# Two layers of linear attention and squared-ReLU FFN on one core: b2 as a weight row, squares on ACT, 32-blocked features, a sum by accumulating DMA, re-placed weight preparation

## The chip, the cores and the metric

The kernel runs on one NeuronCore of a Trainium2 chip. The metric is the device time of one execution in microseconds; the median of three runs of the kernel before is 1429.65 us (1428.79 to 1433.52).

The engines are TensorE (PE, with its weight loads PEld), VectorE (DVE), ScalarE (ACT), GpSimd (POOL) and SyncE (SP, which here only issues DMAs). Each takes its instructions in order; they wait for one another through semaphores.

## The reference

Two layers over x of 2048 tokens by 640 features. One layer is

```python
phi = lambda t: where(t > 0, t + 1, exp(t)) + 1e-6
q, k, v = layernorm(x) @ wqkv            # 32 heads of 20
kv, z = phi(k)^T v, sum_s phi(k)         # per head, over all 2048 tokens
x = x + (phi(q) kv / (phi(q) . z + 1e-6)) @ wo
h = layernorm(x) @ w1 + b1               # 640 -> 1728
x = x + relu(h)**2 @ w2 + b2             # 1728 -> 640
```

Both layers use the same weights, all in float32.

## The kernel before, in words

**Precision.** Every float32 operand of a large product is split into a high part (rounded by an ACT copy to fp32r) and a low part (a DVE subtract); a product is then three fp32r matmuls (`mm3`, L456 to L460). `split` (L121) is the pair of instructions. Splitting is therefore most of the work of ACT and DVE.

**Attention, first stage of a layer** (the loop at L783). The 2048 tokens are 16 tiles of 128. For tile t, x is normalized (`ln_stats`, `ln_apply`; the inverse root is two small POOL instructions, L362 and L363), brought into the transposed layout with the features on the partitions, split (`xT_split`), and multiplied by the resident weights of k and q (`part`, L538). The `Phi` class computes phi: exp on ACT (L555), two DVE instructions for the rest (L562, L563), into a tile from a pool `r` of three buffers. `k_post` (L746) splits phi(k) (low half on DVE at L756) and adds it to the running sum `acc` on POOL (L753; the first tile is a copy, L751). The products with x accumulate in PSUM (`g_part`, `gt_part`). phi(q) is stored to DRAM. For the tiles in `LATE` phi(q) is computed after the loop, in the gaps of the next stage, so these tiles take one `r` buffer instead of two.

**Weight preparation, layer 0 only.** The FFN's weights are split once, stored to DRAM (`kept`), and read from there in both layers. `Prep` (L229) does it inside the attention loop: `load` brings 14 chunks of w1 ("a") and 7 pairs of row tiles of w2 ("t") as scheduled in `PREP`; `mix` (L265, POOL) forms the combinations of w2 that the Winograd form of Strassen's product needs; `high` (ACT, L290) and `low` (DVE, L296) split; `store` (SP, L305, L310) writes the halves. `prep_step` runs four times per tile. The buffers are `g` (raw, four of them) and `u` (split; a ring of six that later holds the FFN weights in flight).

**Middle.** The per-head matrices are formed and multiplied with wo into M; the first four tiles of the attention's output are computed, added to x, normalized and transposed (`x_turned`, `f_trans`), so that the first group of the FFN can start.

**FFN** (the loop at L1388), in four groups g of 512 tokens. FC1 is 14 chunks c of 128 hidden features (`fc1`, L1131), each 15 matmuls into one of four PSUM banks in turn (10 for the last chunk). `act` (L1150) adds b1 and applies ReLU on ACT (L1155) and squares on DVE (L1156) into the array R. Chunk 13 packs the 64 remaining features with their low-order weights. FC2 multiplies R by w2 with seven products instead of eight (`ORDER`, 28 steps n of about 12 matmuls, L1212). `s_op` combines quarters of R in place (DVE, L1173); `u_hi` and `u_lo` split each factor into an arena of five slots (ACT L1192, DVE L1196); `fc2_add` adds finished partial results from PSUM to x (DVE, L1225). The FFN weights stream through the ring `u`, SP loading one when a slot is used up; seven of them (`load_stay`) stay for the layer.

**Side work in the FFN.** While group g is in the FFN, the attention's output for the four tiles of group g+1 is computed by `single(g, i)` (L1276), with its parts placed as events: denominators and scaling on DVE (L689 to L702), a 32x32 block transpose (DVE, L417), 16 block moves (ACT, L426), a split (L1239, L1241), the output product (PE, `out`, into banks 6 and 7, after the chunks in `OUTS`), the residual add (DVE, L1313), statistics and layernorm, a trip through DRAM that does the rest of the transpose (POOL-issued store L389, SP loads L398, DVE `turn` L407), and a split into xTb (`x_split`). `f_bias` (L733) adds b2 to x with a POOL instruction (L736).

**What sets the order.** The schedule is manual: each engine's order is the order in which the code calls. In the FFN it is set by `events`, a table keyed by (g, position) with lists of functions; positions 0 to 13 are the FC1 chunks and 14 + n the FC2 steps. Functions of one position run in the order in which they were registered; before, `single` registers first, then `ffn_events`, then `side_last`.

Of the kernel before, what the change touches and what calls it, by code (L numbers as in the profile page):

```python
# [13 lines left out]
P = 128  # L14
S, D, F = 2048, 640, 1728
H, DH = 32, 20
NT = S // P
# [27 lines left out]
PREP = {2: "aaa", 3: "t", 4: "t", 5: "aaaa", 6: "t", 7: "t", 8: "aaaa", 9: "t", 10: "t", 11: "aaa", 12: "t"}  # L45
# [6 lines left out]
F_BUFS, X_BUFS = 8, 4  # L52
# [12 lines left out]
def kernel(  # L65
# [37 lines left out]
    b2bc = cpool.tile([P, D], F32, name="b2bc")  # L103
    b1sb = cpool.tile([P, NF], F32, name="b1sb")

    def late_consts():
        nc.sync.dma_start(
            b2bc, bass.AP(tensor=b2.tensor, offset=b2.offset, ap=[[0, P], [1, D]])
        )
# [119 lines left out]
    class Prep:  # L229
# [19 lines left out]
        def load_t(self, p):  # L249
            a, b, q = gtile("wa"), gtile("wb"), gtile("wq")  # L250
# [122 lines left out]

    def of_chunk(v, c):

        return v.rearrange("t (p c) -> t c p", c=DC)[:, c]
# [27 lines left out]
    def turn(z):  # L404

        y = ftile("y")
        nc.vector.transpose(  # L407
            out=y.rearrange("p (c i q) -> p i c q", c=DC, q=B32),
            in_=z.rearrange("p (i q c) -> p i c q", c=DC, q=B32),
        )  # L410
        return y
# [100 lines left out]
    for layer in range(N_LAYERS):  # L512
# [213 lines left out]
        def b_x1(t, ps):  # L726
            v = halves_sb(xr[t])
            nc.vector.tensor_tensor(out=v, in0=halves(ps), in1=v, op=ALU.add)
            ln_stats(("b", t), xr[t])
            xn[t] = ftile("xn")  # L730
            ln_apply(("b", t), xn[t], xr[t])

        def f_bias(t):  # L733

            v = xr[t]
            nc.gpsimd.tensor_tensor(out=v, in0=v, in1=b2bc, op=ALU.add)  # L736
# [9 lines left out]
        def k_post(t, r, between=()):  # L746

            kh[t] = u = xtile("kh")
            nc.scalar.activation(u[:, 0], r, AF.Copy)
            if t == 0:  # L750
                nc.gpsimd.tensor_copy(acc, r)  # L751
            else:
                nc.gpsimd.tensor_tensor(out=acc, in0=acc, in1=r, op=ALU.add)  # L753
            for f in between:
                f()
            nc.vector.tensor_tensor(out=u[:, 1], in0=r, in1=u[:, 0].bitcast(F32), op=ALU.subtract)  # L756
# [6 lines left out]
        def x_end(t):  # L763
            return yza.pop(t)[1] if layer == 0 else turn(yza.pop(t))
# [7 lines left out]
        def prep_step(t, i):  # L772
            if layer == 0 and t in PREP_AT:
                if i == 0:
                    prep.mix()
                prep.low()
                prep.high()
                if i == 3:
                    prep.load(PREP.get(t + 1, ""))

        late = LATE[layer]
        q_end = None
        for t in range(NT):  # L783
# [14 lines left out]
            if first:  # L798
# [38 lines left out]
                nc.sync.dma_start(pqd[0], fq.r)  # L837
                continue
# [33 lines left out]
            if early:  # L872
                xT_split(2, turn(yz0[2]))
# [196 lines left out]
        def f_trans(t, ps):  # L1070
            transpose_x(ps, xn.pop(t))
            f_split(t, ps)
# [10 lines left out]
        def x_turned(i):  # L1083

            b_x1(i, po[i])
            yzx[i] = blocks_x(xn.pop(i))
            side_work.extend(lambda k=k: turn_move(yzx[i], (k,)) for k in range(JQ))
            side_work.append(lambda: f_split(i, yzx.pop(i)[1]))
# [9 lines left out]
        wu.free = 3  # L1098
# [27 lines left out]
        nc.gpsimd.memset(R[FL:, :, 1, KH - 1], 0.0)  # L1126
        x1_odd["tile"] = bp.tile([P, TG, D], F32, name="x1", tag="x1", bufs=1)
# [22 lines left out]
        def act(c, ps):  # L1150
# [3 lines left out]
            if c < 13:  # L1154
                nc.scalar.activation(r, v, AF.Relu, bias=b1sb[:, c : c + 1])  # L1155
                nc.vector.tensor_tensor(out=r, in0=r, in1=r, op=ALU.mult)  # L1156
# [119 lines left out]
        def single(g, i):  # L1276
# [3 lines left out]
            def on(n, f):  # L1280
                if n < 0 and g > 0:
                    at(g - 1, NF + N_STEPS + 2 * n, f)
                elif n >= NF:
                    at(g, NF + 2 * (n - NF), f)
                else:
                    at(g, max(n, 0), f)
# [9 lines left out]
            on(b - 3, lambda: next(sp, None))  # L1296
# [13 lines left out]
            def add():  # L1310
# [3 lines left out]
                ln_stats(("b", t), xr[t])  # L1314
                xn[t] = ftile("xn")
                ln_apply(("b", t), xn[t], xr[t])

            at(g, ("pe", b), out)
            on(b + 1, add)

            def store():
                xd[t] = spread_out(xn.pop(t))

            on(b + 1, store)
            on(b + 2, lambda: f_bias(t))
# [8 lines left out]
        def ffn_events(g):  # L1334
            for k in range(PAIRS):
                at(g, 6 + k, lambda k=k: u_hi(g, k))
                at(g, 6 + k, lambda k=k: u_lo(g, k))
            for k in range(3):
                at(g, 9 + 2 * k, lambda k=k: s_op(1, k))
                at(g, NF + k, lambda k=k: s_op(2, k))  # L1340
            at(g, 11, lambda: u_hi(g, PAIRS))
            at(g, 11, lambda: u_lo(g, PAIRS))
            s = NF
            at(g, s, lambda: s_op(1, 3))
            at(g, s + 3, lambda: s_op(2, 3))
            for n in range(PAIRS + 1, N_STEPS):
                at(g, s + n - 4, lambda n=n: u_hi(g, n))
                at(g, s + n - 4, lambda n=n: u_lo(g, n))
            for k in range(PAIRS):
                at(g, s + 6 + k, lambda k=k: s_op(3, k))  # L1350
                at(g, s + 11 + k, lambda k=k: s_op(4, k))
            for q in range(len(ORDER) - 1):
                for i in range(2):
                    at(g, s + PAIRS * (q + 1) + i, lambda q=q, i=i: fc2_add(g, q, i))

        def side_last():
# [20 lines left out]
            for t in range(2):  # L1377
                at(g, s + 8 + 4 * t, lambda t=t: xT_split(t, turn(yz0[t])))

        for g in range(NG):  # L1380
            if g < NG - 1:
                for i in range(TG):
                    single(g, i)
        for g in range(NG):
            ffn_events(g)
        side_last()

        for g in range(NG):  # L1388
            for c in range(NF):
# [5 lines left out]
                if g == 0 and c < TG:  # L1395
                    f_bias(c)
# [50 lines left out]
```

## Time and profile before

| | |
|---|---|
| median of three runs | 1429.65 us |
| the profiled execution | 1429.69 us |
| its span | 1427.7 us |
| instructions | 20898 |
| DMA | 311.41 MB, mean 218 GB/s |
| POOL sums of phi(k), L753 | 54.0 us in 30 instructions |
| POOL adds of b2, L736 | 52.3 us in 32 instructions |
| DVE squares, L1156 | 77.4 us in 104 instructions |

How to read the rows that follow. In a row of a group of instructions stand: line, engine, operation, output and inputs, shape, count, then busy us and the mean ns of one, then the idle time of the engine just before them with what ended it. In a list of waits: total us, times, longest. In a timeline: start, duration, engine, line, operation, count, and in brackets the idle time before it with its releaser. In a table of windows: the length, then each engine's busy time with its count of instructions, the granted TensorE clock (1.00 is full), the DMA engines' busy share and GB/s.

### The profile page before, as it was taken

The page shows a single profiled execution, that of the slowest core. Times are in us where ns is not written, and L with a number is a line of the kernel's source. Part 1 is how long each engine was busy: PE and PEld are TensorE (multiplying, and loading weights), DVE is VectorE, ACT ScalarE, POOL GpSimd, SP SyncE. Part 2 cuts the span into 40 slices and gives each one's busy share as a digit, 9 for nine tenths or more (in the row PEclk, how much of TensorE's full clock was granted, in tenths as well). Part 3 has the DMA queues.
Part 4 walks back from the last instruction along what each step waited for, and adds up shares of the span by engine and source line. Part 5 has one row for each costly group of instructions (what it writes and reads, how often), then busy time and mean ns, then how long its engine had stood idle before and what let it go on. Part 6 is the DMA issues. An engine that isn't in the chain of part 4 may idle for free.

```text
span 1427.7 us, 20898 instructions
## 1 busy us (share of the span) xinstructions
PE 1352.0 (95%) x7525; PEld 1221.1 (86%) x7525; DVE 992.1 (69%) x1679; ACT 662.1 (46%) x1490; POOL 232.2 (16%) x277
## 2 busy tenths in 40 slices
PE   8999889998899899999999999998999999999999
PEld 7877778877898898898988888988789889888888
DVE  7988966855965775783656777676578469559345
ACT  5877766845244435332322322385534443453232
POOL 2433430201101100201002233102020010011000
PEclk9999999999999999999999999999999999999999
DMA  6578793465694496588773334353849738848856
GB/s 194 203 244 296 263 357 110 178 239 195 203 349 176 158 317 222 179 279 335 249 280 111 111 102 143 98 201 129 298 138 305 266 139 274 302 152 238 289 183 221
DMA packets 130044, 311.41 MB, mean 218 GB/s; under 512 B 15558, under 2 KB 60742, under 8 KB 129302
## 3 DMA queue, kind: packets, MB, share of 16 engines
q1 hardware_dynamic: 126742, 296.98, 61.1%
q0 software_dynamic: 3200, 13.11, 2.4%
q8 instruction: 60, 0.98, 0.3%
q14 instruction: 42, 0.34, 0.1%
HBM read 241.83 MB, written 65.54 MB: 215 GB/s over the span
## 4 chain that ended last, share of the span: by engine, by line
PE 53%; DVE 25%; ACT 12%; DMA 4%; issue 4%; POOL 2%; SPq 1%; DVEq 0%; POOLq 0%; ACTq 0%
PE PS L460 22%; PE PS L1212 16%; PE PS L1143 13%; ACT z L426 7%; DVE R L1173 2%; DVE arena L1196 2%; DVE bn L358 2%; DVE pqt L701 2%; DVE R L1156 2%; DMA z<-xb 2%; ACT R L1155 2%; DMA kept<-uprep 1%; DVE x L1313 1%; POOL rs L363 1%; DVE xn L368 1%
## 5 line engine op out<-in xcount | busy, mean ns | idle before, releaser
L1143 PE MATMUL PS<-xTb,u 128*128 128x512 f32 x1640 | 378.5, 391 | 4.3 <-DVE xTb L124 4.3
L1143 PEld LDWEIGHTS PS<-xTb,u 128*128 128x128 f32 x1640 | 307.8, 188 | 67.9 <-DVE xTb L124 4.9
L460 PE MATMUL PS<-kq,xT 128*128 128x320 f32 (+2 forms) x1575 | 288.6, 337 | 12.1 <-DVE GT L593 6.5
L460 PEld LDWEIGHTS PS<-kq,xT 128*128 128x128 f32 x1575 | 253.9, 191 | 41.3 <-issue 7.9
L1212 PE MATMUL PS<-u,arena 128*128 128x320 f32 x1680 | 266.1, 316 | 14.2 <-DVE arena L1196 14.2
L1212 PEld LDWEIGHTS PS<-u,arena 128*128 128x128 f32 x1680 | 257.3, 194 | 16.0 <-DVE arena L1196 15.8
L426 ACT ACTIVATE z<-y 32x160 f32<-32x160 f32 x512 | 171.3, 335 | 163.4 <-DVE y L417 157.4
L1156 DVE TENSOR_TENSOR R<-R 128x512 f32<-128x512 f32 x104 | 77.4, 744 | 172.7 <-ACT R L1155 172.7
L1196 DVE TENSOR_TENSOR arena<-R,arena 128x512 fp32r<-128x512 f32 x224 | 140.0, 634 | 72.0 <-ACT arena L1192 71.3
L1192 ACT ACTIVATE arena<-R 128x512 fp32r<-128x512 f32 x224 | 122.5, 571 | 142.3 <-PE PS L1212 102.7
L362 POOL TENSOR_SCALAR rs<-mv 128x1 f32<-128x1 f32 x64 | 27.5, 429 | 783.2 <-DVE mv L360 783.2
L460 PE MATMUL PS<-uM,pTs 128*128 128x320 f32 x720 | 117.1, 323 | 19.8 <-DVE x L1313 19.7
L460 PE MATMUL PS<-kh,xh 128*128 128x512 f32 x480 | 127.9, 401 | 7.8 <-DVE kh L756 7.8
L460 PEld LDWEIGHTS PS<-uM,pTs 128*128 128x128 f32 x720 | 113.2, 199 | 25.7 <-ACT R L1155 13.5
L1155 ACT ACTIVATE R<-PS,b1sb 128x512 f32<-128x512 f32 x104 | 71.2, 684 | 123.4 <-PE PS L1143 122.8
L555 ACT ACTIVATE e<-PS 128x320 f32<-128x320 f32 (+4 forms) x128 | 53.8, 435 | 149.3 <-PE PS L460 137.0
L1212 PE MATMUL PS<-uw,arena 128*128 128x320 f32 x672 | 109.5, 310 | 4.9 <-DVE x L1225 4.9
L460 PEld LDWEIGHTS PS<-kh,xh 128*128 128x128 f32 x480 | 88.7, 192 | 25.0 <-DVE kh L756 9.6
L1212 PEld LDWEIGHTS PS<-uw,arena 128*128 128x128 f32 x672 | 101.0, 188 | 6.8 <-DVE x L1225 6.5
L446 ACT ACTIVATE z<-y 32x160 f32<-32x160 f32 x272 | 90.8, 334 | 5.6 <-DVE y L432 2.5
L562 DVE TENSOR_SCALAR e<-e 128x320 f32<-128x320 f32 (+4 forms) x128 | 48.6, 380 | 60.6 <-ACT e L555 60.6
L1173 DVE TENSOR_TENSOR R<-R 128x512 f32<-128x512 f32 (+1 forms) x128 | 87.7, 696 | 0.0
(113 smaller groups left out, 1325.8 us busy)
## 6 DMA issues: line engine op xcount, KB each, us to landing
u<-kept SPq DMA_DIRECT2D x112, 640.0 KB, 4.4
u<-kept_w SPq DMA_DIRECT2D x104, 640.0 KB, 5.4
u<-kept SPq DMA_DIRECT2D x56, 320.0 KB, 4.9
kept<-uprep SPq DMA_DIRECT2D x49, 320.0 KB, 5.2
z<-xb SPq DMA_DIRECT2D x160, 80.0 KB, 4.1
pqt<-pq SPq DMA_DIRECT2D x32, 320.0 KB, 4.8
uw<-kept SPq DMA_DIRECT2D x14, 640.0 KB, 6.7
kept_w<-uprep SPq DMA_DIRECT2D x13, 640.0 KB, 6.5
```

Source lines behind the costliest of these rows:

```text
L426: nc.scalar.activation(zv[j * B32 : (j + 1) * B32, :, i, :], yv[i * B32 : (i + 1) * B32, :, j, :], AF.Copy)
L446: nc.scalar.activation(zv[j * B32 : (j + 1) * B32, :, i, :], yv[i * B32 : (i + 1) * B32, j], AF.Copy)
L460: nc.tensor.matmul(ps, a, b, start=first and i == 0, stop=last and i == 2)
L555: nc.scalar.activation(self.e[:, a:b], ps, AF.Exp)
L562: nc.vector.tensor_scalar(e, e, 1.0, PHI_EPS, op0=ALU.min, op1=ALU.add)
L1143: nc.tensor.matmul(ps, a[:, d, :], bb[:, d, :], start=d == 0 and i == 0, stop=d == DC - 1 and i == len(seq) - 1,)
L1155: nc.scalar.activation(r, v, AF.Relu, bias=b1sb[:, c : c + 1])
L1156: nc.vector.tensor_tensor(out=r, in0=r, in1=r, op=ALU.mult)
L1173: nc.vector.tensor_tensor(out=quad(*out, k), in0=quad(*x, k), in1=quad(*y, k), op=op)
L1192: nc.scalar.activation(u[:, 0], v, AF.Copy)
L1196: nc.vector.tensor_tensor(out=u[:, 1], in0=v, in1=u[:, 0].bitcast(F32), op=ALU.subtract)
L1212: nc.tensor.matmul(ps, x, y, start=opens and k == 0 and p == 0 and e == 0, stop=k == PAIRS - 1 and p == b - a - 1 and e == 2, skip_group_c ...
```

## The change

- **b2.** The broadcast load of b2 and the 32 POOL adds are gone. Row 64 of the last, half-empty tile of w2 is loaded with b2, and row 64 of the matching part of R is set to 1.0. One quarter of R is overwritten by `s_op(4)` in each group, so `ones_row` sets it again with two POOL memsets at position 1 of groups 1 to 3.
- **Squares.** ACT squares what its ReLU wrote.
- **Events in the FFN.** `u_lo` moves one position behind its `u_hi`; `s_op(2)` moves from positions 14, 15, 16, 17 to 17 to 20, `s_op(3)` and `s_op(4)` two positions later; the DVE half of the output product's split moves one position later; the layernorm's apply and its store move from b+1 to b+2; the add of the fourth tile moves to FC2 step 1. `ffn_events` registers ahead of `single`.
- **32-blocked features.** In the FFN the features of x are dealt to the partitions in blocks of 32 (partition 32j + p of chunk d holds feature 160j + 32d + p, where before partition p held features 5p to 5p + 4). The DVE transposes then read runs of 32 in place of single elements five apart, `x_turned` uses `blocks_T`, tiles 2 and 3 of group 0 are regrouped by the layernorm's write, and a chunk of w1 is loaded by four DMAs of 32 partitions.
- **Sum of phi(k).** For tiles 1 to 14 POOL issues an accumulating DMA from r to acc. Tile 0 stays a copy and tile 15 an add.
- **Preparation.** The raw buffers become five. Loads are issued at the first of a tile's four sub-steps, a tile ahead; stores at every second sub-step, all but the newest two. The last two pairs of w2 tiles (`LATE_T`) are loaded, mixed, split and stored in the first eleven chunks of layer 0's first FFN group, in memory of R and of the x1 tile that is not used yet; until then the ring loads FC1 weights four ahead instead of six.

The diff, cut to its core:

```diff
-PREP = {2: "aaa", 3: "t", 4: "t", 5: "aaaa", 6: "t", 7: "t", 8: "aaaa", 9: "t", 10: "t", 11: "aaa", 12: "t"}
+PREP = {1: "aa", 2: "aa", 3: "t", 4: "aa", 5: "t", 6: "aa", 7: "t", 8: "aa", 9: "t", 10: "aa", 11: "t", 12: "aa"}
+LATE_T = (5, 6)
-F_BUFS, X_BUFS = 8, 4
+F_BUFS, X_BUFS = 8, 5
...
-            return [(v, w1[:, c * P : c * P + n].rearrange("(p d) f -> p d f", d=DC))]
+            w = w1[:, c * P : c * P + n]
+            return [
+                (v[j * B32 : (j + 1) * B32], w[Q * j : Q * (j + 1)].rearrange("(d p) f -> p d f", p=B32))
+                for j in range(JQ)
+            ]
...
+                nc.sync.dma_start(b[n : n + 1], b2.rearrange("(o n) -> o n", o=1))
...
-        def store(self):
-            while self.done:
+        def store(self, leave=0):
+            while len(self.done) > leave:
...
-    def turn(z):
+    def turn(z, strided=False):
         y = ftile("y")
+        order = "p (i q c) -> p i c q" if strided else "p (i c q) -> p i c q"
...
-        def f_bias(t):
-
-            v = xr[t]
-            nc.gpsimd.tensor_tensor(out=v, in0=v, in1=b2bc, op=ALU.add)
...
             if t == 0:
                 nc.gpsimd.tensor_copy(acc, r)
             else:
-                nc.gpsimd.tensor_tensor(out=acc, in0=acc, in1=r, op=ALU.add)
+                if t < NT - 1:
+                    nc.gpsimd.dma_start(acc, r, accum_op=ALU.add)
+                else:
+                    nc.gpsimd.tensor_tensor(out=acc, in0=acc, in1=r, op=ALU.add)
...
                 if i == 0:
+                    prep.load(PREP.get(t + 1, ""))
                     prep.mix()
                 prep.low()
                 prep.high()
-                if i == 3:
-                    prep.load(PREP.get(t + 1, ""))
+                if i % 2 == 0:
+                    prep.store(2)
...
             if layer == 0:
-                prep.store()
+                if t >= 14:
+                    prep.store()
...
-        wu.free = 3
+        wu.free = 1 if layer == 0 else 3
         wu.load_ring()
...
+        nc.gpsimd.memset(R[FL : FL + 1, :, 1, KH - 1], 1.0)
+        def ones_row():
+            nc.gpsimd.memset(R[FL:, 0, 1, KH - 1], 0.0)
+            nc.gpsimd.memset(R[FL : FL + 1, 0, 1, KH - 1], 1.0)
...
                 nc.scalar.activation(r, v, AF.Relu, bias=b1sb[:, c : c + 1])
-                nc.vector.tensor_tensor(out=r, in0=r, in1=r, op=ALU.mult)
+                nc.scalar.activation(r, r, AF.Square)
...
             on(b - 3, lambda: next(sp, None))
-            on(b - 3, lambda: next(sp, None))
+            on(b - 2, lambda: next(sp, None))
...
-            on(b + 1, add)
-            on(b + 1, store)
-            on(b + 2, lambda: f_bias(t))
+            on(b + 1 + 0.5 * (i == 3), add)
+            on(b + 2, store)
...
                 at(g, 6 + k, lambda k=k: u_hi(g, k))
-                at(g, 6 + k, lambda k=k: u_lo(g, k))
+                at(g, 7 + k, lambda k=k: u_lo(g, k))
...
                 at(g, s + n - 4, lambda n=n: u_hi(g, n))
-                at(g, s + n - 4, lambda n=n: u_lo(g, n))
+                at(g, s + n - 3, lambda n=n: u_lo(g, n))
             for k in range(PAIRS):
-                at(g, s + 6 + k, lambda k=k: s_op(3, k))
-                at(g, s + 11 + k, lambda k=k: s_op(4, k))
+                at(g, s + 3 + k, lambda k=k: s_op(2, k))
+                at(g, s + 8 + k, lambda k=k: s_op(3, k))
+                at(g, s + 13 + k, lambda k=k: s_op(4, k))
...
+        def prep_last():
+            x1 = x1_odd["tile"]
+            h = [R[:, i, 1].rearrange("p c n -> p (c n)")[:, HT + D * j : HT + D * (j + 1)] for i in range(2) for j in range(2)]
+            spots = {5: (x1[:, 2], x1[:, 3], h[0]), 6: (h[1], h[3], h[2])}
+            for i, p in enumerate(LATE_T):
+                at(0, i, lambda p=p: prep.mixes.append(prep.load_t(p, spots[p])))
+                at(0, 1 + 3 * i, prep.mix)
+            def step():
+                prep.low()
+                prep.high()
+                prep.store()
+            for c in range(1, 11):
+                at(0, c, step)
+            at(0, 11, lambda: setattr(wu, "free", wu.free + 2))
```

More of the change, by code (lines that the diff above doesn't have):

```diff
@@ L102 @@
     nc.vector.memset(neghalf, -0.5)
-    b2bc = cpool.tile([P, D], F32, name="b2bc")
     b1sb = cpool.tile([P, NF], F32, name="b1sb")
     def late_consts():
-        nc.sync.dma_start(
-            b2bc, bass.AP(tensor=b2.tensor, offset=b2.offset, ap=[[0, P], [1, D]])
-        )
         with nc.allow_non_contiguous_dma(reason="one bias per partition"):
@@ L372, in transpose5, with by_chunk, by_block @@
             nc.tensor.transpose(ps[:, c * P : (c + 1) * P], src[:, c * P : (c + 1) * P], ident)
+    def by_chunk(v):
+        return v.rearrange("p (c j n) -> p j c n", c=DC, n=B32)
+    def by_block(v):
+        return v.rearrange("p (j c n) -> p j c n", c=DC, n=B32)
     def of_chunk(v, c):
@@ L763, in x_end @@
         def x_end(t):
-            return yza.pop(t)[1] if layer == 0 else turn(yza.pop(t))
+            return yza.pop(t)[1] if layer == 0 else turn(yza.pop(t), True)
         def move(t, n=JQ):
@@ L837 @@
                 nc.sync.dma_start(pqd[0], fq.r)
+                prep.load(PREP[1])
                 continue
@@ L872 @@
             if early:
-                xT_split(2, turn(yz0[2]))
+                xT_split(2, turn(yz0[2], True))
             prep_step(t, 1)
@@ L1377, in side_last @@
             for t in range(2):
[L1378 to L1383, printed above, removed]
+                at(g, s + 8 + 4 * t, lambda t=t: xT_split(t, turn(yz0[t], True)))
         for g in range(NG):
             ffn_events(g)
+        for g in range(NG - 1):
+            for i in range(TG):
+                single(g, i)
         side_last()
+        if layer == 0:
+            prep_last()
         for g in range(NG):
```

30 lines of the change are left out of this document (16 added, 14 removed).

## The prediction

> **What bounds the kernel now.** I read the page's busy shares first, then the waits of PE's matmuls, longest first, then the busy time by stage.
>
> ```profile
> PE 1352.0 (95%) x7525; PEld 1221.1 (86%) x7525; DVE 992.1 (69%) x1679; ACT 662.1 (46%) x1490; POOL 232.2 (16%) x277
> ...
> PE PS L460 <- DVE x L1313: 19.7, 10, 4.7
> PE PS L1212 <- DVE arena L1196: 14.2, 6, 3.3
> PE PS L460 <- DVE kh L756: 7.8, 4, 2.9
> PE PS L460 <- DVE GT L593: 6.5, 1, 6.5
> PE PS L1212 <- DVE x L1225: 4.9, 6, 1.7
> PE PS L1143 <- DVE xTb L124: 4.3, 2, 2.2
> PE PS L460 <- DVE r L563: 4.3, 2, 3.1
> PE PS L460 <- DVE rl L563: 2.5, 2, 1.3
> PE PS L460 <- DMA kq<-kept_kq: 2.5, 1, 2.5
> ```
>
> PE is busy 95% of the span, so the change can win only two things: PE's idle time, 1427.7 - 1352.0 = 75.7 us, and whatever makes its matmuls slow. The waits (total us, times, longest) explain nearly all of the idle time, and eight of these nine rows name DVE, which is itself only 69% busy. DVE has time enough; it is late at certain places.
>
> ```profile
> 0.00:203.00 203.00, 180.60 (x925) 156.39 (x926) 172.45 (x283) 150.15 (x355) 75.45 (x85) 0.96 0.75 253
> ...
> 287.00:739.00 452.00, 428.73 (x2369) 391.25 (x2369) 294.09 (x492) 176.99 (x386) 41.82 (x61) 0.97 0.72 250
> 739.00:905.00 166.00, 166.00 (x878) 145.85 (x879) 123.57 (x223) 50.22 (x94) 50.14 (x54) 0.99 0.37 118
> ...
> 985.00:1427.70 442.70, 420.94 (x2356) 384.62 (x2356) 281.47 (x477) 176.36 (x384) 36.51 (x49) 0.98 0.68 233
> ...
> 174.73 1.63 PE L460 MATMUL PS<-kh,xh 128*128 128x512 f32 x4 [2.11 <-DVE kh L756]
> ...
> 175.30:178.70 3.40, 3.40 (x12) 3.00 (x11) 3.05 (x4) 1.48 (x5) 0.83 (x2) 0.50 1.02 279
> ```
>
> The columns are PE, PEld, DVE, ACT and POOL busy, granted clock, DMA share and GB/s. The first four rows are layer 0's attention, its FFN, layer 1's attention and its FFN. Layer 1's attention has no idle PE at all, 166.00 of 166.00. A part of the change that works only there wins nothing. The last two rows show the second loss: after a pause of 2.11 us the clock stood at 0.50 for the next 3.4 us. Over the four stages the clock shares give 0.04 x 203 + 0.03 x 452 + 0.01 x 166 + 0.02 x 442.7 = 32 us of lost clock. [...]
>
> **The change part by part.** *Squares on ACT, split products one event later, FFN events ahead of side work.* This is the chain that holds PE in FC1:
>
> ```profile
> 331.74 2.75 ACT L426 ACTIVATE z<-y 32x160 f32<-32x160 f32 x8
> ...
> 339.31 0.68 DVE L1156 TENSOR_TENSOR R<-R 128x512 f32<-128x512 f32 x1
> 339.91 0.88 DVE L1313 TENSOR_TENSOR x<-PS,x 128x320 f32<-128x320 f32 x2
> 340.55 1.67 PE L460 MATMUL PS<-uM,pTs 128*128 128x320 f32 x5 [4.67 <-DVE x L1313]
> ...
> L1192 ACT ACTIVATE arena<-R 128x512 fp32r<-128x512 f32 x168 | 104.2, 625 | 109.0 <-PE PS L1212 92.6 <-DVE x L1225 9.0 <-DVE R L1173 6.9
> L1156 DVE TENSOR_TENSOR R<-R 128x512 f32<-128x512 f32 x104 | 77.4, 744 | 172.7 <-ACT R L1155 172.7
> ```
>
> The next tile's output product needs the PSUM banks that the residual add (L1313) reads. On DVE the add stands behind the square of its chunk (L1156), the square behind ACT's Relu, the Relu behind block moves of 2.75 us. DVE waited 172.7 us in total for the Relu. With the square on ACT, DVE has nothing in FC1 that waits for the current chunk's Relu; it can reach the add as soon as the previous product is done. It loses 104 x 0.744 = 77 us of work. ACT gains 104 squares; I price one at the 625 ns of the nearest row, another SBUF to SBUF activation of that shape, so 65 us in all and 13 x 0.625 = 8.1 us in each FC1 pass. What that leaves:
>
> ```profile
> 1218.00:1276.00 58.00, 57.94 (x291) 50.08 (x290) 29.68 (x48) 29.75 (x75) 6.12 (x8) 1.00 0.62 234
> ```
>
> In this FC1 pass ACT was busy 29.75 of 58.00 us, so about 38 afterwards: the work fits. The Relus are not urgent, since PE uses four banks in turn and asks for a bank again only three chunks later (58.00 / 14, some 4 us a chunk with the four output products counted in). Behind a square on ACT's queue wait the next split, block moves and half of the product's split; each has at least one chunk in hand. The 19.7 us (L1313) should go.
>
> *b2 as a weight row.* It removes 32 adds on POOL and one load, and adds one row of 1.0 by small memsets. The adds take POOL time that nobody waits for, yet they cost DVE:
>
> ```profile
> 361.78 2.59 DVE L1196 TENSOR_TENSOR arena<-R,arena 128x512 fp32r<-128x512 f32 x1
> 362.23 1.59 POOL L736 TENSOR_TENSOR x<-x,b2bc 128x640 f32<-128x640 f32 x1
> ...
> 279.79 6.95 POOL L736 TENSOR_TENSOR x<-x,b2bc 128x640 f32<-128x640 f32 x4
> 279.98 1.66 DVE L562 TENSOR_SCALAR e<-e 128x320 f32<-128x320 f32 x1
> ...
> 286.86 5.31 PE L1143 MATMUL PS<-xTb,u 128*128 128x512 f32 x15 [2.17 <-DVE xTb L124]
> ```
>
> A split subtract that meets the add takes 2.59 us. That delay sits where FC2 begins (arena, 14.2) and, four adds in a row, just before FC1 begins (xTb 4.3, rl 2.5). After the change no POOL arithmetic is left at either place. Together with the reordering I take 38.8 us of FFN waits (19.7 + 14.2 + 4.9) down to 4: some of the 4.9 (L1225) is DVE being full in the middle of FC2, and the combines moved later there only spread it. So 35 us are saved. Of the 6.8 at the start of FC1, 1.3 stay, because the last tile's split follows its transpose as before: 5.5 saved.
>
> *phi(k) summed by DMA, weight preparation re-placed.* In layer 0's attention:
>
> ```profile
> 128.17 0.74 ACT L290 ACTIVATE uprep<-st 128x640 fp32r<-128x640 f32 x1 [6.04 <-DMA kept<-uprep]
> ...
> 184.57 2.11 POOL L753 TENSOR_TENSOR acc<-acc,r 128x640 f32<-128x640 f32 x1
> 185.22 2.15 DVE L296 TENSOR_TENSOR uprep<-wq,uprep 128x640 fp32r<-128x640 f32 x1
> ...
> 188.31 4.07 PE L460 MATMUL PS<-kq,xT 128*128 128x320 f32 x14 [6.52 <-DVE GT L593]
> ```
>
> Two causes show. ACT sat 6.04 us for a store to free a preparation buffer, with the exponentials behind it; and POOL's sum slows DVE just before k's low half. Stores are now issued every second sub-step instead of in one burst per tile, and 28 of the 30 sums leave POOL. Two of seven mixed tiles leave the stage. But the stage stays dense (DVE 172.45 of 203 us), so of 7.8 + 6.5 + 4.3 = 18.6 us I keep 5 and save 13.6. In layer 1 the same edit saves nothing (no idle PE there).
>
> The accumulate itself is shown by no row. Its bounds:
>
> ```profile
> xb<-xt POOLq DMA_DIRECT2D x16, 320.0 KB, 2.6
> ...
> kept_kq<-kq SPq DMA_DIRECT2D x10, 640.0 KB, 8.4
> ...
> 86.22 1.62 POOL L753 TENSOR_TENSOR acc<-acc,r 128x640 f32<-128x640 f32 x1 [10.38 <-DVE r L563]
> ...
> 99.76 1.68 POOL L753 TENSOR_TENSOR acc<-acc,r 128x640 f32<-128x640 f32 x1
> ```
>
> A POOL-queued write of the same size lands in 2.6 us; the slowest ordinary copy takes 8.4. Each issue also waits on POOL for the previous sum to land; behind it stands the small layernorm pair that the next tile needs a step later. The tile r that it reads is rewritten by phi(q) of the next step, one step on, 99.76 - 86.22 = 13.5 us. Anywhere between the bounds it costs nothing. [...]
>
> W1 is now loaded by four DMAs a chunk instead of one, 42 more issues on SP in layer 0:
>
> ```profile
> 26.17 2.11 SPq L244 DMA_DIRECT2D st<-in_B_w_dram  x3
> ```
>
> At 0.70 us each that is 29 us of SP over a stage of 203; the x loads queued behind are asked for three tiles ahead, so I count nothing. Without that lead it would be at most 8 x 0.70 = 5.6 us per step.
>
> The two tiles moved into the first FFN group of layer 0 each bring two loads, seven stores, four POOL mixes, four splits on ACT and DVE:
>
> ```profile
> kept<-uprep SPq DMA_DIRECT2D x49, 320.0 KB, 5.2
> ...
> 290.00:340.00 50.00, 45.25 (x217) 38.27 (x215) 26.55 (x41) 24.85 (x62) 3.16 (x4) 0.98 0.76 276
> ...
> 320.00:325.00 5.00, 4.38 (x29) 4.02 (x28) 3.90 (x10) 0.00 (x0) 1.56 (x3) 1.00 1.02 390
> ```
>
> That is 2 x 9 x 0.32 = 5.8 MB more in a stretch that moved 276 GB/s x 50 us = 13.8 MB; 19.6 MB at the 390 GB/s of a full window need 50 us. So the DMA engines are just full there, while the ring of FC1 weights runs four chunks ahead instead of six and SP's stores wait for DVE's low halves with ring loads behind them. Eight ACT splits of 0.74 us and the squares bring ACT near 44 of 58 us (29.75 + 8.1 + 5.9), and a split may wait for its buffer. Cost between 0 and 10 us (PE late by two to three landings); I take 3, nearer to the lower end because four chunks are some 16 us and landings some 5.
>
> The FFN's block transposes lose their strided read, and the layernorm's write is regrouped: less DVE work or the same, nothing on the path; counted zero.
>
> [...]
>
> **Sum.** 35 + 5.5 + 13.6 + 24 - 3 = 75.1. Against the profiled execution, 1429.69 us (span 1427.7; the median of the runs is 1429.65, the same), that gives 1354.6.
>
> **The rivals.** *(a) Half of the FFN waits come back through ACT.* ACT now holds Relu, square, split, moves; if a move waits for DVE's block transpose, all of these stand behind. For it: ACT's splits and moves already gate DVE. Against it: 38 of 58 us busy. Half of 38.8 and of the preparation's 18.6 stays, with half of the clock loss: saved (19.4 + 5.5 + 9.3 + 12) - 6 = 40, so 1390.
>
> [...]
>
> *(c) Slower: the accumulate holds r.* If it lands after L us, L > 13.5, DVE stands at phi(q) of the next step in 16 steps (tiles 2 to 8 and 10 of layer 0, 2 to 7, 10 and 12 of layer 1), and PE, which has no slack in layer 1, with it: 16 x (L - 13.5). It eats the 75 us from L = 18.2; at L = 20 it is 104 us and the time 1459. The rows nearest, 2.6 and 8.4, are far below.
>
> **How the numbers follow.** Forecast 1354 with 0.66, (a) 0.20, (b) 0.09, (c) 0.05. The range reaches down to 1337, where all waits (38.8 + 6.8 + 18.6) and 28 of the clock go and nothing is added, 92 us, and up to 1392, which takes in (a) and (b). A measurement of this kernel tells about 0.3% from no change, 4 us. Faster by more: 0.92, within: 0.03, slower: 0.05.
>
> **What would show it.** Right: no wait of L460 for the FFN's residual add, none of L1212 for arena above 1 us; layer 0's attention stage near 185 us instead of 203; clock 0.99 over the span; split subtracts all near 0.7 us in the FFN; accumulates landing within 10 us. Wrong: PE waits that name ACT's split or a ring load between layer 0's first FC1 chunks 4 and 13, DVE idle for the accumulate at phi(q), or ACT waiting for stores of prepared weights.

## The result, and the profile after

The changed kernel takes 1367.33 us (median of 4 runs, 1366.55 to 1372.08) against 1429.22 us of the kernel before: a ratio of 0.9577, 95% interval 0.9536 to 0.9617. Its profiled execution has a span of 1365.8 us, 61.9 us less than before, and a mean granted clock of 0.994 (before: 0.978).

Line numbers shift with the change. L470 is `mm3` (L460 before), L1163 FC1, L1232 FC2, L1216 `u_lo`, L1333 the residual add, L1245 `fc2_add`, L573 the last step of phi, L767 the low half of phi(k), L120 and L121 `split`, L292 and L298 `Prep.high` and `low`.

First the busy shares of the page after, and two of its groups: the products' low halves and the squares on ACT.

```profile
PE 1330.0 (97%) x7525; PEld 1204.4 (88%) x7525; DVE 851.2 (62%) x1575; ACT 733.6 (54%) x1594; POOL 163.4 (12%) x259
...
L1216 DVE TENSOR_TENSOR arena<-R,arena 128x512 fp32r<-128x512 f32 x224 | 137.3, 617 | 139.3 <-ACT arena L1212 138.5
```

```profile
L1176 ACT ACTIVATE R<-R 128x512 f32<-128x512 f32 x104 | 65.8, 633 | 3.3
```

PE's idle time went from 75.7 to 35.8 us. Where it still waits, by the list of PE's waits (total us, times, longest), for two stretches: layer 0's attention, 0 to 225 us, and everything from the start of the first FFN on.

```profile
PE PS L470 <- DVE r L573: 15.2, 6, 3.6
PE PS L470 <- DVE xT L121: 3.2, 3, 2.4
...
PE PS L470 <- DVE kh L767: 1.2, 1, 1.2
PE PS L470 <- DVE GT L603: 1.0, 2, 0.6
```

```profile
PE PS L470 <- DMA kq<-kept_kq: 1.9, 1, 1.9
PE PS L1232 <- ACT xT L120: 1.7, 1, 1.7
PE PS L1163 <- DVE xTb L121: 1.0, 2, 0.5
```

The three FFN rows of before (19.7, 14.2 and 4.9 us) are gone: nothing in the second list names the residual add, the arena or `fc2_add`. In the first list the order is turned round: kh and GT are small, and r, which cost 4.3 us before, costs 15.2.

The table by stage, of before and then of after. The boundaries are the first matmul on `acc` (the sum of phi(k) is finished, so layer 0's attention loop is over), the first of FC1, the same two in layer 1, and the end; the columns are those of the tables of windows in the prediction.

```profile
0.00:219.87 219.87, 197.47 (x1025) 172.10 (x1026) 182.46 (x299) 155.09 (x363) 79.48 (x87) 0.96 0.76 259
219.87:286.86 66.99, 62.70 (x412) 57.32 (x410) 51.71 (x91) 50.46 (x129) 10.62 (x13) 1.00 0.37 134
286.86:918.28 631.42, 608.15 (x3325) 549.70 (x3326) 424.81 (x724) 229.89 (x485) 95.07 (x116) 0.98 0.62 211
918.28:985.22 66.94, 62.70 (x412) 57.33 (x410) 51.83 (x91) 50.33 (x129) 10.61 (x13) 1.00 0.37 134
985.22:1427.70 442.48, 420.94 (x2356) 384.62 (x2356) 281.25 (x476) 176.36 (x384) 36.41 (x48) 0.98 0.68 233
```

```profile
0.00:225.03 225.03, 200.10 (x1024) 172.26 (x1025) 159.13 (x291) 150.31 (x355) 55.19 (x78) 0.96 0.79 246
225.03:288.82 63.79, 62.38 (x413) 57.16 (x411) 48.03 (x91) 50.37 (x129) 4.43 (x10) 1.00 0.34 120
288.82:886.49 597.67, 593.43 (x3325) 538.66 (x3326) 365.90 (x680) 270.26 (x545) 76.63 (x119) 1.00 0.73 243
886.49:950.41 63.92, 62.39 (x412) 57.17 (x410) 48.15 (x91) 50.36 (x129) 4.43 (x10) 1.00 0.39 140
950.41:1365.80 415.39, 411.70 (x2356) 379.14 (x2356) 230.00 (x424) 212.29 (x436) 22.72 (x42) 1.00 0.73 249
```

So the first FFN with layer 1's attention won 33.8 us, the second FFN 27.1, the two middles 3.2 and 3.0, and **layer 0's attention loop lost 5.2**, though DVE and POOL have 23 and 24 us less to do in it. Its clock is still 0.96.

What holds that loop is seen in ACT's waits there, one row of before (0 to 220 us) and two of after (0 to 225 us), and in one of the pauses of after in order of time.

```profile
ACT uprep L290 <- DMA kept<-uprep: 14.5, 3, 6.0
```

```profile
ACT uprep L292 <- DMA st<-in_B_w_dram: 23.7, 13, 4.5
ACT uprep L292 <- DMA wb<-in_B_w_dram: 18.8, 5, 4.6
```

```profile
99.72 1.03 SPq L257 DMA_DIRECT2D wb<-in_B_w_dram  x1
...
105.65 0.74 ACT L292 ACTIVATE uprep<-wb 128x640 fp32r<-128x640 f32 x1 [4.30 <-DMA wb<-in_B_w_dram]
...
106.30 0.72 ACT L120 ACTIVATE xT<-z 128x640 fp32r<-128x640 f32 x1
...
107.05 1.16 DVE L121 TENSOR_TENSOR xT<-z,xT 128x640 fp32r<-128x640 f32 x1 [4.52 <-ACT xT L120]
...
109.21 0.29 DVE L573 SCALAR_TENSOR_TENSOR r<-PS,e 128x128 f32<-128x128 f32 x1
...
110.84 1.97 PE L470 MATMUL PS<-xh,kh 128*128 128x320 f32 x6 [3.60 <-DVE r L573]
```

SP issues a raw weight at 99.72. ACT's next instruction is the split of that weight; it stands 4.30 us until the load has landed. Behind it on ACT is the split of xT, then DVE's half, the exponentials, phi, and PE after a pause of 3.60 us. PE's list names r because r comes last in this chain; its first link is a load. The waits for stores (14.5 us before, of which the prediction showed the 6.04) are indeed gone after; 23.7 + 18.8 = 42.5 us for loads came in their place. In the changed code `prep_step` calls `prep.load` in sub-step 0 and, in the same sub-step, `mix` and `high`, which take what has just been asked for. "A tile ahead", as the change was described above, holds only for the index in `PREP`; before, the load stood in sub-step 3 and its use in the next tile.

### The profile page after: what moved, and what is told of

Its sections match the earlier page's. It is cut to its first block, busy times and chain, and to the rows that moved or that the text cites. A ratio compares the mean times of both kernels' runs of the same rounds, so it can differ in the third digit from the quotient of the medians.

```text
span 1365.8 us, 20962 instructions
## 1 busy us (share of the span) xinstructions
PE 1330.0 (97%) x7525; PEld 1204.4 (88%) x7525; DVE 851.2 (62%) x1575; ACT 733.6 (54%) x1594; POOL 163.4 (12%) x259
## 4 chain that ended last, share of the span: by engine, by line
PE 75%; DVE 9%; DMA 6%; ACT 5%; issue 2%; SPq 2%; POOL 0%; DVEq 0%; ACTq 0%; POOLq 0%
PE PS L1163 27%; PE PS L470 23%; PE PS L1232 23%; ACT z L456 2%; DMA wb<-in_B_w_dram 2%; SPq L245 1%; DVE uprep L298 1%; DMA u<-kept 1%; ACT z L436 1%; DVE bn L360 1%; DMA st<-in_B_w_dram 1%; DVE e L572 1%; DVE r L573 1%; DMA kq<-kept_kq 1%; DVE xh L121 1%
## 5 line engine op out<-in xcount | busy, mean ns | idle before, releaser
L1163 PE MATMUL PS<-xTb,u 128*128 128x512 f32 x1640 | 376.9, 390 | 1.0 <-DVE xTb L121 1.0
L1163 PEld LDWEIGHTS PS<-xTb,u 128*128 128x128 f32 x1640 | 306.7, 188 | 64.0 <-DVE xTb L121 1.5
L470 PE MATMUL PS<-kq,xT 128*128 128x320 f32 (+2 forms) x1575 | 288.0, 337 | 4.7 <-DMA kq<-kept_kq 1.9
L470 PEld LDWEIGHTS PS<-kq,xT 128*128 128x128 f32 x1575 | 252.8, 190 | 34.9 <-DMA kq<-kept_kq 2.3
L1232 PE MATMUL PS<-u,arena 128*128 128x320 f32 x1680 | 256.3, 309 | 2.1 <-ACT xT L120 1.7
L1232 PEld LDWEIGHTS PS<-u,arena 128*128 128x128 f32 x1680 | 248.8, 188 | 2.8 <-ACT xT L120 2.0
L1216 DVE TENSOR_TENSOR arena<-R,arena 128x512 fp32r<-128x512 f32 x224 | 137.3, 617 | 139.3 <-ACT arena L1212 138.5
L1212 ACT ACTIVATE arena<-R 128x512 fp32r<-128x512 f32 x224 | 126.3, 573 | 155.7 <-PE PS L1232 147.9
L470 PE MATMUL PS<-kh,xh 128*128 128x512 f32 x480 | 128.5, 402 | 3.9 <-DVE xT L121 2.4
L470 PE MATMUL PS<-uM,pTs 128*128 128x320 f32 x720 | 109.4, 309 | 0.0
L470 PEld LDWEIGHTS PS<-uM,pTs 128*128 128x128 f32 x720 | 107.5, 188 | 1.9
L1232 PE MATMUL PS<-uw,arena 128*128 128x320 f32 x672 | 107.8, 309 | 0.0
L470 PEld LDWEIGHTS PS<-kh,xh 128*128 128x128 f32 x480 | 89.1, 193 | 20.9 <-DVE kh L767 2.8
L1232 PEld LDWEIGHTS PS<-uw,arena 128*128 128x128 f32 x672 | 101.0, 188 | 0.2
L364 POOL TENSOR_SCALAR rs<-mv 128x1 f32<-128x1 f32 x64 | 35.3, 552 | 530.3 <-DVE mv L362 530.3
L1193 DVE TENSOR_TENSOR R<-R 128x512 f32<-128x512 f32 (+1 forms) x128 | 78.5, 618 | 27.7 <-ACT R L1176 27.7
L572 DVE TENSOR_SCALAR e<-e 128x320 f32<-128x320 f32 (+4 forms) x128 | 44.5, 347 | 62.1 <-ACT e L565 61.9
L1245 DVE TENSOR_TENSOR x<-PS,x 128x320 f32<-128x320 f32 x112 | 53.9, 486 | 22.7 <-PE PS L1232 22.7
```

The source lines that it names most:

```text
L470: nc.tensor.matmul(ps, a, b, start=first and i == 0, stop=last and i == 2)
L572: nc.vector.tensor_scalar(e, e, 1.0, PHI_EPS, op0=ALU.min, op1=ALU.add)
L1163: nc.tensor.matmul(ps, a[:, d, :], bb[:, d, :], start=d == 0 and i == 0, stop=d == DC - 1 and i == len(seq) - 1,)
L1193: nc.vector.tensor_tensor(out=quad(*out, k), in0=quad(*x, k), in1=quad(*y, k), op=op)
L1212: nc.scalar.activation(u[:, 0], v, AF.Copy)
L1216: nc.vector.tensor_tensor(out=u[:, 1], in0=v, in1=u[:, 0].bitcast(F32), op=ALU.subtract)
```

## The experiments

The theory after the result had three parts: (1) the loads without lead cost layer 0's attention some 20 us; (2) the FFN's gain is shared by squares, order of events and b2 row; (3) the accumulating DMA is worth little. Six experiments take one part back or cure it in the changed kernel (one of them in its cured version), three do one part alone in the kernel before, and one builds on the cured version.

**The load after the splits** (changed kernel, two lines of `prep_step`):

```diff
                 if i == 0:
-                    prep.load(PREP.get(t + 1, ""))
                     prep.mix()
                 prep.low()
                 prep.high()
+                if i == 0:
+                    prep.load(PREP.get(t + 1, ""))
```

> The changed kernel with one move: in layer 0's attention the raw weight loads are issued behind the first sub-step's mix, low and high instead of ahead of them, so nothing asks for a load in the sub-step that issues it. Theory (ACT stands still for loads that were only just issued: 23.7 + 18.8 us of ACT waits on raw weights, and PE's 15.2 us on phi follow): ACT's waits for raw weights fall below 10 us, PE's idle time in layer 0's attention below 8 us, time 1345 to 1352 against 1367. Rival (that stage is held by DVE's and POOL's density, the loads only coincide): time 1362 or more, PE's waits there still 12 us or more.

Measured: 1347.64 us, ratio 0.9435 (0.9405 to 0.9465), faster than both kernels. ACT's waits of 0 to 200 us, then the first stage:

```profile
ACT uprep L292 <- DMA st<-in_B_w_dram: 6.9, 3, 4.2
```

```profile
0.00:199.76 199.76, 191.31 (x1024) 168.53 (x1025) 158.15 (x291) 150.02 (x355) 58.66 (x78) 0.99 0.86 271
```

The waits for raw weights fall from 42.5 to 6.9 us and the stage from 225.03 to 199.76; PE's idle time in it is 199.76 - 191.31 = 8.45 us, a little over the 8 that was expected; the next stretch, the first FFN with layer 1's attention, takes 3.2 us more (600.88), which the last experiment takes up. So the loss was the missing lead, and without it the stage is 20.1 us faster than before, about what the prediction had asked of it (13.6 us and its share of the clock).

**Squares back on DVE** (changed kernel; the line `nc.scalar.activation(r, r, AF.Square)` becomes the DVE product of before).

> The changed kernel with FC1's squares back on DVE, all else as changed. Theory (the square behind ACT's ReLU is what made DVE late for the residual add): the waits of the output product for the residual add come back, 10 to 20 us in total with 5 to 10 us of clock, time 1380 to 1395. Rival (POOL's b2 adds and the order of events were the cause, squares not): time 1371 or less, no such waits.

Measured: 1385.07 us, ratio 0.9698 (0.9668 to 0.9728): 18 us slower than the changed kernel. The time is the one that the theory gave, the wait is not: the residual add (x) stands at 2.3 us instead of 10 to 20, and the new FFN row is the low half of the output product's split:

```profile
PE PS L470 <- DVE pTs L1261: 8.8, 6, 1.7
...
PE PS L470 <- DVE x L1333: 2.3, 1, 2.3
```

**Only the squares on ACT** (the kernel before with that one line changed).

> The kernel before with FC1's squares moved to ACT and nothing else. Theory (squares, POOL's adds and the order of events each hold a part of the FFN's waits): 8 to 20 us faster than before, 1408 to 1420, since DVE still meets ACT in the same event for every split and POOL's adds still stretch it. Rival (the squares alone free DVE): 35 us or more faster, 1393 or less.

Measured: 1421.99 us (10 runs), ratio 0.9964 (0.9949 to 0.9980). Both expectations missed: the move alone is worth 0.4%. PE's waits, then DVE's waits (first one row of the kernel before), then one of them in order of time:

```profile
PE PS L460 <- DVE x L1313: 19.6, 8, 4.5
PE PS L1212 <- DVE x L1225: 10.7, 7, 2.5
...
PE PS L1212 <- DVE arena L1196: 7.3, 5, 2.7
```

```profile
DVE arena L1196 <- ACT arena L1192: 71.3, 55, 3.5
```

```profile
DVE arena L1196 <- ACT arena L1192: 165.9, 77, 25.2
DVE pTs L1241 <- ACT pTs L1239: 117.6, 24, 9.1
```

```profile
328.63 2.75 ACT L426 ACTIVATE z<-y 32x160 f32<-32x160 f32 x8
331.39 0.63 ACT L1192 ACTIVATE arena<-R 128x512 fp32r<-128x512 f32 x1
...
332.06 0.69 DVE L1196 TENSOR_TENSOR arena<-R,arena 128x512 fp32r<-128x512 f32 x1 [7.62 <-ACT arena L1192]
...
336.86 0.88 DVE L1313 TENSOR_TENSOR x<-PS,x 128x320 f32<-128x320 f32 x2
337.49 3.68 PE L460 MATMUL PS<-uM,pTs 128*128 128x320 f32 x13 [3.38 <-DVE x L1313]
```

The residual add's wait is what it was (19.7, now 19.6). DVE no longer stands for the Relu (172.7 us before); it stands for the high halves, 165.9 and 117.6 us, where before it was 71.3 us for the first and nothing for the second. The add is queued behind the `u_lo` of the two positions before it, with a product's split and the next denominators between them. The first of these `u_lo` waits 7.62 us for ACT's copy, which stands behind the block moves; from there DVE works on to the add with one more wait, 1.18 us for the split. `fc2_add` waits more than before (10.7 us, 4.9 before). The wait has gone to other instructions of the same queue.

**The old order of FFN events** (changed kernel, the event positions and the order of registration of before).

```diff
-                at(g, 7 + k, lambda k=k: u_lo(g, k))
+                at(g, 6 + k, lambda k=k: u_lo(g, k))
...
-                at(g, s + n - 3, lambda n=n: u_lo(g, n))
+                at(g, s + n - 4, lambda n=n: u_lo(g, n))
...
-            on(b + 1 + 0.5 * (i == 3), add)
+            on(b + 1, add)
```

> The changed kernel with the FFN's events as before: split subtracts in the event of their high part, the combines, the product's split, the residual add and the layernorm at their old positions, side work registered first. Squares stay on ACT, b2 a weight row. Theory (the order carries what the squares' 18 us and the POOL adds' 8 us leave of the FFN's and the middle's 66 us): 15 to 35 us slower than the changed kernel, 1382 to 1402. Rival (with the squares gone the order no longer matters): 1371 or less.

Measured: 1410.94 us (6 runs, 1403.37 to 1414.12), ratio 0.9891 (0.9857 to 0.9926), 43 us slower than the changed kernel by the medians and more than expected; the profiled run, the fastest, is 36 us slower. The rows of both adds are back, and the ring runs late:

```profile
PE PS L470 <- DVE x L1333: 10.5, 7, 2.6
PE PS L1232 <- DVE x L1245: 8.5, 7, 1.8
PE PS L1163 <- DMA u<-kept_w: 7.1, 3, 4.5
```

**Only the order** (the kernel before with the event edits alone; the `s_op` of the expectation are the combinations of quarters of R).

> The kernel before with one part of the change alone: the order of the FFN events (each u_lo one step later, the LayerNorm sums s_op later, split, add and store one or two steps later, the list of FFN events written ahead of the attention's). Squares stay on DVE, b2 stays with POOL, phi(k) is summed by POOL, weights are prepared as before. Theory after the runs that undid or did one part: the order is what took most of the FFN's waits away, because the changed kernel with the old order lost 43 us and the squares alone won 6; alone it gives 1395 to 1412 us, with DVE waits in the FFN down from 38.8 to under 15. Rival: the order pays only where DVE has been unburdened (squares away, POOL adds away), then it gives 1415 us or more and the FFN waits stay over 25.

Measured: 1396.32 us, ratio 0.9758 (0.9731 to 0.9785): the order alone wins more than any other part, with squares and b2 adds left where they were. Its waits in the FFN:

```profile
PE PS L460 <- DVE pTs L1241: 12.7, 10, 1.7
...
PE PS L1212 <- DVE arena L1196: 5.0, 8, 1.0
```

and its longest wait of DVE:

```profile
DVE R L1156 <- ACT R L1155: 224.0, 82, 6.4
```

12.7 + 5.0 = 17.7 us instead of 38.8, a little above the 15 that the theory gave; the add (L1313) and `fc2_add` (L1225) are gone from the list. What is left, pTs, is the row that came back when the squares returned to DVE, so it is most likely the part that the squares pay for. DVE stands longer for the Relu than in the kernel before, 224.0 us against 172.7, and the kernel is 2.4% faster all the same: most of that idle time did not hold PE.

**Only the b2 row** (the kernel before with b2 in w2, without the 32 POOL adds).

> The kernel before with b2 as a weight row and its POOL adds gone, nothing else. Theory (POOL's adds stretch DVE at the start of FC1 and of FC2): 8 to 20 us faster, 1408 to 1420, arena waits below 5 us. Rival (as the zero adds cost the changed kernel only 8 us, they are worth no more here): 1418 to 1424, arena waits above 8 us.

Measured: 1404.28 us, ratio 0.9836 (0.9808 to 0.9865), better than expected. No wait for the arena is left (14.2 before) and little at the start of FC1 (xTb and rl, 6.8 before, now 1.7). But `fc2_add` rises from 4.9 to 13.4 us, so 8.5 of the arena's 14.2 only went to another instruction; the residual add falls from 19.7 to 13.3 (lines are two to four lower here):

```profile
PE PS L1210 <- DVE x L1223: 13.4, 7, 2.5
PE PS L457 <- DVE x L1311: 13.3, 10, 2.7
...
PE PS L1141 <- DVE xTb L120: 1.0, 2, 0.5
```

**POOL adds back** (changed kernel with 32 POOL adds of a zero tile at the places of the b2 adds; the sum computed is the same).

> The changed kernel with 32 POOL adds of a tile of zeros to x where b2 was added before; b2 itself stays a weight row, so the result is the same. Theory (POOL's two-input adds stretch DVE where FC2 and FC1 begin): split subtracts beside an add take over 1.5 us, arena and xTb waits return, 5 to 15 us with clock, time 1373 to 1385. Rival (with the squares gone from DVE there is slack enough): time 1366 to 1370, stretched instructions but no PE waits.

Measured: 1375.61 us, ratio 0.9626 (0.9598 to 0.9654), 8 us slower than the changed kernel by the medians; the intervals of the two ratios just overlap. The low halves take 668 ns on average instead of 617 (the longest 2.68 us), and the start of FC1 waits again. The arena waits do not return (0.3 us), against the theory:

```profile
L1222 DVE TENSOR_TENSOR arena<-R,arena 128x512 fp32r<-128x512 f32 x224 | 148.6, 668 | 137.2 <-ACT arena L1218 136.6
```

```profile
PE PS L1169 <- DVE xTb L123: 3.6, 2, 2.2
```

**phi(k) summed by POOL again**, once in the changed kernel and once in the one with the late loads.

> The changed kernel with the sum of phi(k) by POOL adds again, all else as changed. Theory (the loads hold layer 0's attention, the sum is beside the path; layer 1 is full either way): 0 to 6 us slower, 1367 to 1373, the loss in layer 0's attention alone. Rival one (the POOL sum was half of that stage's waits): 10 us or more slower. Rival two (the accumulating DMA itself costs time there): faster by 3 us or more.

> The first experiment (raw loads issued behind the sub-step's splits, 1347.6) with the sum of phi(k) by POOL adds again. Theory (once no load holds ACT, the POOL sum's stretching of DVE is next): PE waits on kh or r come back in layer 0's attention, 3 to 12 us slower, 1350 to 1360. Rival (the stage has slack for it): 1346 to 1349.

Measured: 1369.89 us (0.9586, 0.9557 to 0.9616), which can't be told from the changed kernel, and 1352.40 us (0.9471, 0.9444 to 0.9498), 4.8 us above the kernel with the late loads by the medians (the intervals of the ratios overlap; the single runs, 1350.88 to 1352.98 and 1345.08 to 1348.84, do not). In the profiles 4.9 us of the difference lie in layer 0's attention (199.76 to 204.65 at its first matmul on `acc`). The accumulating DMA is worth some 5 us, but only once the loads no longer hide it.

**The z loads earlier** (the version with the late loads; the loads of z for layer 1's first three tiles, four DMAs each, move from FC2 into FC1 of the last group, chunks 10 to 12).

```diff
-                at(g, s + 2 + 3 * t, lambda t=t: load(t))
+                at(g, 10 + t, lambda t=t: load(t))
```

> The changed kernel with the late weight loads, and with the next layer's four loads of z moved from the steps of FC2 into FC1 of the last group (chunks 10 to 13). In the version with late weight loads alone SP stood 5.75 us at the four loads (649.22 to 654.97), and FC2 after it waited 2.1 and 2.4 us for ring weights and for kq. Theory: those waits and the clock drop behind them go, 1343 to 1346 us beside 1347.6. Rival: the four loads only move the jam into FC1, where the weights of w1 stream too; 1347 to 1350 us, with the ring waits then in FC1.

Measured: 1341.41 us (1341.30 to 1345.87), ratio 0.9375 (0.9352 to 0.9398), the fastest of all and a little below what the theory gave. SP's issue of one tile's four DMAs, the slowest of three such in the version with the late loads, then one of this version:

```profile
649.22 5.75 SPq L407 DMA_DIRECT2D z<-xb  x4
```

```profile
623.89 1.80 SPq L407 DMA_DIRECT2D z<-xb  x4
```

The stretch from the first FC1 to the end of layer 1's attention loop takes 596.56 us instead of 600.88, and the other stages agree within 0.4 us, so the gain (1343.3 to 1339.6 in the spans) is where the edit is: the waits there for ring weights (2.5) and for the arena (0.7) are gone. The wait for kq at the start of layer 1 is not (2.4, now 2.8), nor the drop of the clock behind it (0.97 from 640 to 690 us, now 0.96 from 640 to 686); in that the theory was wrong.

## Why the prediction was right or wrong

| step of the sum | predicted | measured | how |
|---|---|---|---|
| waits in the FFN, 38.8 | 35 | 37.1 | 1.7 left (xT, at the end of layer 0's FFN) |
| start of FC1, 6.8 | 5.5 | 5.0 | 1.0 (xTb) and 0.8 (rl) left |
| layer 0's attention, 18.6 | 13.6 | -2.0 | 15.2 (r) + 3.2 (xT) + 1.2 (kh) + 1.0 (GT) = 20.6 now |
| clock | 24 | 23.2 | 0.022 x 1427.7 = 31.4 before, 0.006 x 1365.8 = 8.2 now |
| two late tiles of w2 | -3 | 0 | no idle PE in their stretch (below) |
| sum | 75.1 | 63.3 | spans: 61.9 |

**The step that failed** is the 13.6 us of layer 0's attention. Its reasons, "Stores are now issued every second sub-step instead of in one burst per tile, and 28 of the 30 sums leave POOL", hold, and the waits for stores went. But the loads were taken to be a tile ahead and nothing was charged for them. They are used in the sub-step that issues them, and ACT stands 42.5 us for them. None of the signs of being wrong looked there: they name stores, ring loads and the accumulate. It is the whole miss: 13.6 + 2.0 = 15.6 us too much there, against 3 for the late tiles and small terms the other way. With two lines moved the kernel takes 1347.64 us, 7 us under the forecast, and the stage wins 20.1 us.

**The clock's term** came out in size (23.2 for 24), but no run shows the 24 themselves; what the runs show is a mean granted clock of 0.978 before and 0.994 after. By stage, the attention shows 0.96 before and after, and the FFN's two stretches went from 0.98 to 1.00.

**The FFN's size was right, its cause was not,** so that the 37.1 us beside the 35 are partly luck: all the parts were in the kernel together. "With the square on ACT, DVE has nothing in FC1 that waits for the current chunk's Relu; it can reach the add as soon as the previous product is done" names the wrong instruction. DVE has `u_lo` and pTs in front of the add, and they wait for the same ACT. The single parts show it: alone, order -2.4%, b2 row -1.6%, squares -0.4%, together 4.4% where the whole change has 4.2% with the loss in the attention, and 67.1 us or 4.7% without that stage; taken back from the changed kernel, order +3.1%, squares +1.2%, POOL adds +0.5% of the time before (differences of the ratios). So the order carries most of it, and the squares pay more with the other parts in place, most likely because pTs has then become the late one. The idle time of 172.7 us that the prediction read as the price of the Relu was hardly one: with it gone DVE's waits for ACT's high halves rose from 71.3 to 283.5 us, and with the order alone changed it grew to 224.0 us in a faster kernel.

**b2** went as argued at the start of FC1: the edit alone takes the two middles from 66.99 and 66.94 us to 64.34 and 64.39, most of what the whole change wins there. At the start of FC2 it is half the story: the arena's 14.2 us go, but 8.5 of them come back at `fc2_add`, and with the order and the squares changed the POOL adds bring no arena wait. The size alone was not given in the prediction; it is 1.6%.

**The late tiles** are free. The stretch from 290 to 390 us holds them, 952 to 1052 is the same stretch of layer 1 without them:

```profile
290.00:390.00 100.00, 100.00 (x573) 91.91 (x572) 69.11 (x124) 63.57 (x135) 15.65 (x23) 1.00 0.94 336
952.00:1052.00 100.00, 100.00 (x575) 92.16 (x574) 63.56 (x117) 59.54 (x127) 7.30 (x14) 1.00 0.79 268
```

The DMA engines are nearly full (0.94), as was worked out, but PE is busy throughout and no wait for the ring stands there. A square takes 633 ns where 625 was taken from the nearest row.

**The rivals.** (a), waits returning through ACT, came in the FFN with 1.7 us only (xT); ACT did become the engine that holds PE, but in the attention, and by a load. (b), to which the chances give 0.09, expected the clock not to recover; it went from 0.978 to 0.994. (c), the accumulate holding r: the page's row gives the landing as

```profile
acc<-r POOLq DMA_DIRECT2D x28, 320.0 KB, 4.3
```

and the slowest of the 28 took 9.5 us, over the 8.4 that the prediction took as the upper bound (the loads of wo already took 8.9 in the kernel before) and under the 13.5 us of the window. Of the signs named, the 185 us for the attention failed; clock 0.99, no FFN waits for the add, low halves near 0.7 us (at most 0.694) and landings under 10 us came.

Left open: the parts overlap, so no exact share can be given to each; which of the order's moves does it, since no run separates them; what the 32-blocked features are worth, which no run takes back; and the wait for kq at the start of layer 1 (1.9 to 2.8 us in the changed kernel and its variants) was not cured.

## What to carry to other kernels

Ask of an engine that takes its instructions in order not what its longest wait is for, but what stands right ahead of the urgent instruction and whether that has its data; taking away the longest wait alone handed most of the time to other instructions fed by the same producer here, while re-placing instructions in the queue, the second half of a producer-consumer pair one step later among them, took no work away and won most. For every load that is moved, write down the sub-step that issues it and the one that first uses it, in the order of the calls: an index that says "next tile" is no lead. And test parts both ways, alone and taken back: the squares were worth 0.4% one way and 1.2% the other.

## What the runs showed of the hardware

**The clock fell by windows, not by pauses.** In the profiled executions of before and after, the drops to half clock begin at whole multiples of about 3.41 us from one another (after: 31.8, 52.3, 110.3, 141.0 and 171.7 us, that is 6, 17, 9 and 9 windows apart) and last 3.41 us, some of those of before twice that. Laid on that grid, with PE's idle time in a window summed from the matmuls' starts and modelled ends and windows already at half clock left out: with 2.0 us of idle time or more the next window was slow in all of 18 cases, with 1.6 to 2.0 in 1 of 4, with less than 1.6 in none of 765. Hence a pause of 2.29 us that falls across two windows, 1.19 and 1.10 us, cost nothing (before, at 88.8 us; the clock stays at 1.00), and one of 2.11 us inside one cost 1.7 us more (before, at 172.6 us; 0.50 for the next 3.41 us).

**An accumulating DMA from SBUF to SBUF** of 320 KB landed in 4.3 us (median of the changed kernel's 28; 3.6 to 9.5), and POOL needed 0.92 us (median) to issue it in place of an add of 1.68 us (median, before). DVE's low half of phi(k) takes 823 ns on average in the changed kernel and 995 with the POOL sum back in it, the low half of x that stands next to it 816 and 1257.

**SP was held in the middle of its issues.** One tile's four DMAs of 80 KB cost SP 5.75 us in one place and 1.80 us in another (the last experiment). In the changed kernel three such sets took 1.81, 1.83 and 5.42 us (at 663.30, 669.32 and 673.15 us); 3.83 us of the longest lie between its first and second issue, and what is queued behind the four on SP begins at 678.67. SP's waits from 660 to 690 us put 3.8 us in one piece on the landing of a load of kq, which SP had issued 5.48 us before the first of the four. In the version with the late loads a load of kq was issued 5.44 us before the slow set (643.78 and 649.22), so most likely it held SP there too. A full share of the DMA engines alone did not do it: it was 1.05 during the 5.42 us, and 1.06 during the 1.83.
